# Attention and MLP on one core: key blocks of 64 for 58 queries, reciprocals spread by TensorE for eight pairs, query group sums on GpSimd at first

## The chip, the cores and the metric

The kernel runs on one core of a Trainium2 chip. The metric is the device time of one execution in microseconds (us). A profiled execution gives a trace; its span is about 1.7 us shorter than the time of the same execution. Executions are sorted into fast and slow (slow: over 1.5% above the fastest of the same kernel), and ratios use fast ones alone.

## The reference, cut to what matters

```python
# q, k, v: 8 batches x 8 heads x 576 x 64; x: 4608 x 512; w_in 512 x 2048; w_out 2048 x 512
q_d, k_d, v_d = means over groups of 4 neighbours        # 144 rows
out_d   = softmax(scale * q_d @ k_d.T) @ v_d             # then each row repeated 4 times
scores  = where(|i - j| < 4, scale * q @ k.T, -1e9)
x       = repeat(out_d, 4) + softmax(scores) @ v         # all heads beside each other
out     = silu(x @ w_in) @ w_out
```

So each head has a narrow band (each query sees seven keys) and a coarse attention over 144 averaged rows. Both softmaxes need their denominators' reciprocals, spread over the 64 rows of a head before the product P·V is scaled.

## The kernel before: the parts that matter here

Two heads (a "pair") are worked on at a time, 32 pairs in all. TensorE's queue holds transposes (T), scores (S), denominators (Z), P·V (PV), sums of v (VP), the spreading of the reciprocals (RB) and the MLP (g1 = x·w_in, g2 = g·w_out). In the long loop T(n+1), S(n), Z(n−1) and PV(n−2), of four neighbouring pairs, form one burst V(n), followed by four g1 and four g2.

```python
NDIR = 4                                   # pairs whose reciprocals TensorE spreads; the others go through DRAM
...
def pe_S(u, p):                            # 6 blocks: 64 keys for 48 queries
    for i in range(6):
        for h in range(2):
            for y in range(2):
                t = 288 * y + 48 * i
                mm(u, AB[half(y), h, 48 * i:48 * i + 48], kT[j][half(h), t:t + 64], qT[j][half(h), t:t + 48], rl, [rAB[h]])
    ...                                    # 8 more for the coarse scores
def pe_main(u, pv, z):
    for s in range(8):                     # denominators: 36 columns at a time, one-hot weights
        for h in range(2):
            for j in range(2):
                mm(u, CD[half(h), j, 360:396], oh1[half(j), 63 - s:127 - s] if s else ohf[half(j), :],
                   Pt[m][half(j), h, 36 * s:36 * s + 36], ...)
    ...                                    # coarse denominators, P.V in 6 blocks of 48, coarse P.V
def after_Z(p):
    one("DVE", f"r{p}", 0.75, lambda e: e.reciprocal(zr[i][:, :, :], CD[:, :, 360:396]), ...)   # 72 columns
    if p < NDIR:
        return
    dma(... scr[u] <- zr[i] ...)           # to DRAM and back, every row read by 64 partitions
def RB(p):                                 # 20 fp32 matmuls of 36 columns, weights = selectors
    for x in range(2):
        for m in range(10):
            mm(u, HP[:, x, 36 * m:36 * m + 36], sel[:, m, :], zr[i][:, x, :], ...)
...
for name in "T0 T1 S0 T2 S1 Z0 RB0 VP0 T3 S2 Z1 PV0 RB1 VP1 S3 Z2 PV1 RB2 VP2 Z3 PV2 RB3 VP3 PV3".split():
    ...                                    # prologue; then pairs 4 to 9 with the first 16 g1 between
for n in range(10, 46):                    # the loop: burst, then 4 g1 and 4 g2
    if n < NPAIR + 2:
        V(n)
        feed()
    G1(1); g2(j, tt, 0, bank, rb); G1(1); g2(j, tt, 1, bank, rb)
    G1(1); g2(j, tt, 2, bank, rb); g2(j, tt, 3, bank, rb); G1(1)
```

A planner then orders the units by estimated times; every engine executes its own list in that order.

The softmax here doesn't subtract the row's maximum and nothing guards it: scores larger than these inputs give would overflow.

Of the kernel before, what the change touches and what calls it, by code (L numbers as in the profile page):

```python
# [19 lines left out]
NDIR = 4  # L20
# [238 lines left out]
def bass_hourglass_attn__then__act_silu_kernel(  # L259
# [9 lines left out]
    with kctx:  # L269
# [22 lines left out]
        vs = sb("vs", [128, 12, 64], F32, NVS)  # L292
# [3 lines left out]
        vb = sb("vb", [128, 12, 64], BF16, NV)  # L296
# [7 lines left out]
        zr = sb("zr", [128, 2, 36], F32, 2)  # L304
        Rb = sb("Rb", [128, 720], F32, NR)
        xo = sb("xo", [128, 2, 360], F32, NX)
        scr = [nc.dram_tensor(f"scr{i}", [128, 72], F32, kind="Internal").ap() for i in range(NR)]

        sel = gT[1][:, 0:5, :].bitcast(F32).rearrange("p a (y m) -> p (a y) m", m=128)
        selr = [R(f"g1_{f}") for f in range(5)]  # L310
# [6 lines left out]
        pb = sb("pb", [128, 132], BF16)  # L317

        AB = E(nc.psum_tensor("AB", [128, 2, 512], F32))
        CD = E(nc.psum_tensor("CD", [128, 2, 512], F32))  # L320
# [5 lines left out]
        rCD = [R("C", True), R("D", True)]  # L326
# [22 lines left out]
        rc = R("xo1")  # L349

        def constants():
            def pool(fn, r=(), w=(), cost=0.3):
                one("POOL", "const", cost, fn, r, w)

            s, rid = cf[:, 0:64], R("cf")
            pool(lambda g: g.memset(s, 0.0), w=[rid], cost=0.15)
            for j in range(2):
                pool(lambda g, j=j: g.affine_select(out=s, in_=s, compare_op=ALU.not_equal, fill=1.0, base=-64 * j,
                                                    pattern=[[-1, 64]], channel_multiplier=1), r=[rid], w=[rid])
            pool(lambda g: g.tensor_copy(idn[:, :], s), r=[rid], w=[R("id"), R("xo1")], cost=0.2)  # L360

        def constants2():
            def pool(fn, r=(), w=(), cost=0.3):
                one("POOL", "const", cost, fn, r, w, prio=30)

            for i in range(NT):
                for a, b in ((0, 8), (584, 592)):
                    pool(lambda g, i=i, a=a, b=b: g.memset(kT[i][:, a:b], 0.0), w=[R(f"kTp{i}{a}")], cost=0.1)
                pool(lambda g, i=i: g.memset(kd[i][:, 144:192], 0.0), w=[R(f"kdp{i}")], cost=0.1)
            for i in range(NVQ):  # L370
                for s in (1, 3):
                    pool(lambda g, i=i, s=s: g.memset(vq[i][:, s, :], 0.0), w=[R(f"vqc{i}{s}")], cost=0.25)
            pool(lambda g: g.memset(oh1[:, :], 0.0), w=[R("oh1a")], cost=0.15)
            pool(lambda g: g.memset(oh4[:, :], 0.0), w=[R("oh4a")], cost=0.15)
            pool(lambda g: g.memset(ohc[:, :], 0.0), w=[R("ohca")], cost=0.15)
            pool(lambda g: g.memset(oh1[:, 63:64], 1.0), r=[R("oh1a")], w=[R("oh1")], cost=0.1)
            pool(lambda g: g.memset(ohf[:, :], 1.0), w=[R("ohfa")], cost=0.1)
            pool(lambda g: g.memset(ohf[:, 1:10], 0.0), r=[R("ohfa")], w=[R("ohf")], cost=0.1)
            pool(lambda g: g.memset(oh4[:, 63:64], 4.0), r=[R("oh4a")], w=[R("oh4")], cost=0.1)
            for j in range(2):  # L380
                one("DVE", "const", 0.1, lambda g, j=j: g.memset(ohc[64 * j:64 * j + 16, 63:64], 4.0),
                    r=[R("ohca")], w=[R(f"ohc{j}")])
            cf2 = xo[0][:, :, :].rearrange("p a b -> p (a b)")
            rm = R("cm")
            pool(lambda g: g.memset(cf2[:, 0:576], 1.0), w=[rm], cost=0.4)
            for j in range(2):
                s = cf2[:, 288 * j:288 * j + 288]
                m = s.rearrange("p (i q) -> p i q", i=6)
                pool(lambda g, m=m, j=j: g.affine_select(
                    out=m, in_=m, compare_op=ALU.is_ge, fill=0.0, base=-5 - 64 * j,  # L390
                    pattern=[[0, 6], [-1, 48]], channel_multiplier=1), r=[rm], w=[rm], cost=0.5)
                pool(lambda g, m=m, j=j: g.affine_select(
                    out=m, in_=m, compare_op=ALU.is_ge, fill=0.0, base=11 + 64 * j,
                    pattern=[[0, 6], [1, 48]], channel_multiplier=-1), r=[rm], w=[rm], cost=0.5)
                e = s[:, 240 * j:240 * j + 48]
                pool(lambda g, e=e, j=j: g.affine_select(
                    out=e, in_=e, compare_op=ALU.is_ge, fill=0.0, base=119 if j else -8,
                    pattern=[[0, 48]], channel_multiplier=-1 if j else 1), r=[rm], w=[rm])
            pool(lambda g: g.memset(sel[:, :, :], 0.0), w=selr, cost=0.8)
            for j in range(2):  # L400
                pool(lambda g, j=j: g.affine_select(
                    out=sel[:, :, half(j)], in_=sel[:, :, half(j)], compare_op=ALU.not_equal, fill=1.0,
                    base=-64 * j, pattern=[[-1, 10], [0, 64]], channel_multiplier=1), r=selr, w=selr, cost=0.9)
            pool(lambda g: g.memset(pb[:, :], 0.0), w=[R("pba")], cost=0.1)
            pool(lambda g: g.memset(cf2[:, 576:600], 1.0), w=[R("cp")], cost=0.1)
            for j in range(2):
                s = cf2[:, 576 + 12 * j:588 + 12 * j]
                pool(lambda g, s=s, j=j: g.affine_select(
                    out=s, in_=s, compare_op=ALU.is_ge, fill=0.0, base=-8 - 64 * j,
                    pattern=[[-4, 12]], channel_multiplier=1), r=[R("cp")], w=[R("cp")], cost=0.15)  # L410
                pool(lambda g, s=s, j=j: g.affine_select(
                    out=s, in_=s, compare_op=ALU.is_ge, fill=0.0, base=11 + 64 * j,
                    pattern=[[4, 12]], channel_multiplier=-1), r=[R("cp")], w=[R("cp")], cost=0.15)
            for j in range(2):
                one("DVE", "const", 0.1, lambda e, j=j: e.tensor_copy(
                    pb[half(j), 60:72], cf2[half(j), 576 + 12 * j:588 + 12 * j]), r=[R("cp"), R("pba")],
                    w=[R(f"pb{j}"), R("xo0")])
            for j in range(2):
                one("DVE", "const", 0.25, lambda e, j=j: e.tensor_copy(
                    mask_bf[half(j), :], cf2[half(j), 288 * j:288 * j + 288]), r=[rm], w=[R(f"mask{j}"), R("xo0")])  # L420
# [20 lines left out]
        def load_v(p):  # L441
            i = p % NVS
            for h in range(2):
                n = 2 * p + h
                base = v[n // H_, n % H_]
                for j in range(2):
                    lo, hi = 0, 6
                    off = (288 * j - 8) * D_
                    w = [R(f"vs{i}{h}{j}")]
                    d = vs[i][half(j), 6 * h:6 * h + 6, :]  # L450
                    if n == 0 and j == 0:
                        lo = 1
                        one("DVE", "zero", 0.15, lambda g, d=d: g.memset(d[:, 0, :], 0.0), w=w)
                        first = bass.AP(tensor=base.tensor, offset=base.offset, ap=[[64, 56], [1, 64]])
                        dma("SP", f"lv{p}e", vs[i][8:64, 0, :], first, w, f"vs{i}{h}{j}", 0.1, prio=10 * p + 15)
                    if n == 2 * NPAIR - 1 and j == 1:
                        hi = 5
                        last = bass.AP(tensor=base.tensor, offset=base.offset + 520 * D_, ap=[[64, 56], [1, 64]])
                        dma("SP", f"lv{p}e", vs[i][64:120, 11, :], last, w, f"vs{i}{h}{j}", 0.1, prio=10 * p + 15)
                    win = bass.AP(tensor=base.tensor, offset=base.offset + off + 3072 * lo,  # L460
                                  ap=[[64, 64], [3072, hi - lo], [1, 64]])
                    dma("SP", f"lv{p}", d[:, lo:hi, :], win, w, f"vs{i}{h}{j}", 0.55, prio=10 * p + 15)
# [42 lines left out]
        def castw(p):  # L505
            i, m = p % NVS, p % NV
            rr = [R(f"vs{i}{h}{j}") for h in range(2) for j in range(2)]
            one("POOL", f"cw{p}", 0.85, lambda g: g.tensor_copy(vb[m][:, :, :], vs[i][:, :, :]), r=rr, w=[R(f"vb{m}")])  # L508
# [20 lines left out]
        def after_T(p):  # L529
# [7 lines left out]
                kT[j][:, 8:584].rearrange("p (g r) -> p g r", r=9),  # L537
# [3 lines left out]
                kd[j][:, 0:SD], kT[j][:, 8:584].rearrange("p (g r) -> p g r", r=4), AX.X, ALU.add),  # L541
                r=[R(f"kT{j}")], w=[R(f"kd{j}")])
            one("DVE", f"mq{p}", 0.74, lambda e: e.tensor_reduce(  # L543
                qd[j][:, :], qT[j][:, :].rearrange("p (g r) -> p g r", r=4), AX.X, ALU.add),
                r=[R(f"qT{j}")], w=[R(f"qd{j}")])
# [373 lines left out]
```

## Time and profile before

| | before |
|---|---|
| median of 4 runs beside the changed kernel (range) | 437.4 us (433.9 to 443.4) |
| profiled run | 444.3 us, span 442.6 us, mean granted TensorE clock 0.942, slow |
| prologue / loop / tail of that span | 116.4 / 243.1 / 83.1 us |

Beside the lines that the prediction shows, two more of the page are needed. The first is VectorE's busy share in 40 equal slices of 11 us (9 is 90% or more); the second a group of instructions: busy us, mean ns of one, idle time just before.

```profile
DVE  5532125576555464656464656566776543433420
...
L666 DVE RECIPROCAL zr<-CD 128x72 f32<-128x72 f32 x32 | 19.4, 607 | 50.9 <-PE CD L336 50.9
```

VectorE is nowhere over 80% busy: it stands at 1 to 3 tenths in the slices from 22 to 66 us, where three of the four RB blocks lie.

### The profile page before, as it was taken

Reading aid. Unit: us, or ns where it says so; the run is one execution under the profiler, and the core shown is the slowest. Engines: PE = TensorE matmul, PEld = TensorE weight load, DVE = VectorE, ACT = ScalarE, POOL = GpSimd, SP = SyncE. Lnnn points to the kernel's source line nnn. Section 1 sums busy time; section 2 is a strip of 40 time slices with the busy share of each in tenths; the row PEclk is TensorE's granted clock in tenths of the full one; section 3 lists DMA queues with packets and bytes.
Section 4 is the critical chain, followed back from the end, with each engine's and each line's share of the span. In section 5 each row is a group of like instructions: output and inputs, shape, how many; then the busy total and the mean of one; then the engine's idle time right before and its main releaser. Section 6 shows DMA issues by size and latency. Waiting matters only on the chain.

```text
span 442.6 us, 14638 instructions
## 1 busy us (share of the span) xinstructions
PE 384.9 (87%) x6530; PEld 265.3 (60%) x6560; DVE 221.0 (50%) x355; ACT 169.1 (38%) x290; POOL 166.2 (38%) x207
## 2 busy tenths in 40 slices
PE   2799987974597887969797989799999999999997
PEld 1799985653464554646465656466666656666653
DVE  5532125576555464656464656566776543433420
ACT  4221024532244251524344445354545434343421
POOL 9441224356634444445354545445632120000000
PEclk9999999889589896969698999999999999999999
DMA  8999909978997474746575767583131210110111
GB/s 224 262 275 279 211 8 204 254 184 238 215 269 208 125 219 123 198 141 187 146 191 160 204 185 221 152 209 111 67 97 63 87 62 28 43 49 24 49 47 71
DMA packets 87258, 67.35 MB, mean 152 GB/s; under 512 B 59036, under 2 KB 68764, under 8 KB 87196
## 3 DMA queue, kind: packets, MB, share of 16 engines
q1 hardware_dynamic: 74460, 48.77, 41.9%
q10 hardware_dynamic: 8512, 11.36, 9.1%
q0 software_dynamic: 4224, 6.29, 6.6%
q8 instruction: 51, 0.84, 0.8%
q14 instruction: 11, 0.09, 0.1%
HBM read 58.03 MB, written 10.47 MB: 155 GB/s over the span
## 4 chain that ended last, share of the span: by engine, by line
PE 82%; issue 7%; DMA 4%; DVE 2%; ACT 2%; ACTq 1%; SPq 0%; DVEq 0%
PE HP L336 40%; PE o L336 23%; PE CD L336 8%; PE pe_ L336 6%; DMA scr<-zr 2%; PE AB L336 2%; PE pe_ L526 1%; DMA Rb<-scr 1%; DMA qk<-in_k_dram 1%; ACTq L425 1%; PE o L526 1%; ACT th L738 1%; DVE zr L666 1%; DVE gT L740 0%; SPq L425 0%
## 5 line engine op out<-in xcount | busy, mean ns | idle before, releaser
L336 PE MATMUL HP<-xT,w_in_sb 128*128 128x512 f32 x576 | 177.7, 447 | 2.7 <-DVE gT L740 2.3
L740 DVE SCALAR_TENSOR_TENSOR gT<-th,HP 128x512 bf16<-128x512 f32 x144 | 97.1, 685 | 119.3 <-ACT th L738 118.8
L738 ACT ACTIVATE th<-HP 128x512 f32<-128x512 f32 x144 | 85.8, 598 | 160.1 <-PE HP L336 150.1
L336 PEld LDWEIGHTS HP<-xT,w_in_sb 128*128 128x128 f32 x576 | 114.4, 204 | 34.1 <-DVE gT L740 3.2
L336 PE MATMUL o<-w_out_bf,gT 128*128 128x512 bf16 x437 | 106.4, 386 | 2.5 <-issue 1.0
L336 PEld LDWEIGHTS o<-w_out_bf,gT 128*128 128x128 bf16 x464 | 42.0, 100 | 60.0 <-issue 17.6
L722 POOL TENSOR_TENSOR xT<-xo 128x576 fp32r<-128x576 f32 (+3 forms) x48 | 45.0, 950 | 74.0 <-DVE xo L695 74.0
L508 POOL CAST vb<-vs 128x768 bf16<-128x768 f32 x32 | 26.4, 826 | 97.5 <-PE CD L336 88.5
L666 DVE RECIPROCAL zr<-CD 128x72 f32<-128x72 f32 x32 | 19.4, 607 | 50.9 <-PE CD L336 50.9
L502 POOL CAST qkb<-qk 128x1152 bf16<-128x1152 f32 x30 | 34.4, 1146 | 25.1 <-PE pe_ L526 13.2
L336 PE MATMUL CD<-Pt,vb 64*64 64x48 bf16 x768 | 14.8, 196 | 24.7 <-issue 24.4
L336 PE MATMUL HP<-zr,gT 128*128 128x36 f32 x160 | 35.0, 408 | 0.2 <-DVE zr L666 0.2
L336 PEld LDWEIGHTS HP<-zr,gT 128*128 128x128 f32 x160 | 34.4, 332 | 0.6 <-DVE zr L666 0.3
L695 DVE TENSOR_TENSOR xo<-CD,Rb 128x720 f32<-128x720 f32 x32 | 28.7, 898 | 11.7 <-PE CD L336 9.7
L513 POOL TENSOR_TENSOR vt<-vq 128x512 f32<-128x512 f32 x24 | 30.8, 1283 | 0.0
L536 ACT ACTIVATE kT<-pe_ 128x576 bf16<-128x576 bf16 x32 | 20.8, 650 | 18.9 <-PE pe_ L526 11.2
L755 ACT ACTIVATE osb<-o 128x512 f32<-128x512 f32 x29 | 17.4, 599 | 26.4 <-PE o L336 26.2
L336 PEld LDWEIGHTS CD<-Pt,vb 64*64 64x64 bf16 x768 | 11.1, 117 | 26.5 <-issue 25.4
L336 PE MATMUL pe_<-w_out_bf,gT 128*128 128x512 bf16 x109 | 26.1, 380 | 0.2
L540 DVE TENSOR_REDUCE kd<-kT 128x144 bf16<-128x576 bf16 x32 | 23.6, 738 | 1.7 <-ACT kT L536 1.7
L526 PE MATMUL o<-idn,qkb 64*64 64x64 bf16 x576 | 17.8, 206 | 7.6 <-DVE qkb L497 6.0
L543 DVE TENSOR_REDUCE qd<-qT 128x144 bf16<-128x576 bf16 x32 | 23.8, 743 | 1.3 <-ACT qT L339 1.2
(69 smaller groups left out, 358.3 us busy)
## 6 DMA issues: line engine op xcount, KB each, us to landing
vs<-in_v_dram SPq DMA_DIRECT2D x126, 96.0 KB, 4.1
Rb<-scr ACTq DMA_DIRECT2D x56, 180.0 KB, 4.1
qk<-in_q_dram SPq DMA_DIRECT2D x32, 288.0 KB, 5.5
out_dram<-osb SPq DMA_DIRECT2D x36, 256.0 KB, 2.3
qk<-in_k_dram SPq DMA_DIRECT2D x31, 288.0 KB, 6.0
vq<-in_v_dram SPq DMA_DIRECT2D x24, 256.0 KB
w_in_sb<-in_moe_w_in_dram POOLq DMA_DIRECT2D x4, 1024.0 KB, 10.0
w_out_bf<-in_moe_w_out_dram POOLq DMA_DIRECT2D x4, 512.0 KB, 9.9
```

The source lines that it names most:

```text
L336: L.op(u, lambda t: t.matmul(out_, lhsT, rhs, start=start, stop=stop, skip_group_check=True), r, w)
L502: one("POOL", f"c{p}", 1.15, lambda g: g.tensor_copy(qkb[j][:, :, :], qk[i][:, :, :]), r=[R(f"qk{i}0"), R(f"qk{i}1")], w=[R(f"qkb{j}0"), R ...
L508: one("POOL", f"cw{p}", 0.85, lambda g: g.tensor_copy(vb[m][:, :, :], vs[i][:, :, :]), r=rr, w=[R(f"vb{m}")])
L513: one("POOL", f"va{p}", 1.3, lambda g: g.tensor_tensor(vt[:, :, :], vq[i][:, :, 0:128], vq[i][:, :, 128:256], ALU.add), r=rr, w=[R("vt")])
L526: L.op(u, lambda e, o=o, w=w, j=j: e.transpose(o, w, idn[half(j), :]), [R("id"), R(f"qkb{n}{x}")], [rE if x else rF])
L540: one("DVE", f"mk{p}", 0.74, lambda e: e.tensor_reduce(kd[j][:, 0:SD], kT[j][:, 8:584].rearrange("p (g r) -> p g r", r=4), AX.X, ALU.add), ...
L543: one("DVE", f"mq{p}", 0.74, lambda e: e.tensor_reduce(qd[j][:, :], qT[j][:, :].rearrange("p (g r) -> p g r", r=4), AX.X, ALU.add), r=[R(f ...
L666: one("DVE", f"r{p}", 0.75, lambda e: e.reciprocal(zr[i][:, :, :], CD[:, :, 360:396]), r=rCD, w=[R(f"zr{i}")], prio=-4)
L695: one("DVE", f"m{p}", 0.92, lambda e: e.tensor_tensor(xo[x][:, :, :].rearrange("p x (m n) -> p x m n", n=36), CD[:, :, 0:360].rearrange("p ...
L722: one("POOL", f"a{p}", 0.15 + n * 0.0019, lambda g, dst=dst, in0=in0, in1=in1: g.tensor_tensor(dst, in0, in1, ALU.add), r=[R(f"xo{x}")], w ...
L738: one("ACT", f"t{j}_{f}", 0.62, lambda e: e.activation(th[tb][:, :], hps[hb], AF.Tanh, scale=0.5), r=[rH[hb]], w=[R(f"th{tb}")], prio=-1)
L740: one("DVE", f"s{j}_{f}", 0.71, lambda e: e.scalar_tensor_tensor(gT[j % 2][:, f, :], th[tb][:, :], 1.0, hps[hb], ALU.add, ALU.mult), r=[rH ...
```

## The change

Intent: fewer and wider TensorE instructions in the burst (58 queries a block; denominators 72 columns at a time), a cheap RB for eight pairs in place of a dear one for four, and a prologue in which T, S, Z, PV and RB of neighbouring pairs alternate.

```diff
-NDIR = 4
+NDIR = 8
-        vb = sb("vb", [128, 12, 64], BF16, NV)
+        vb = sb("vb", [128, 10, 64], BF16, NV)
-        zr = sb("zr", [128, 2, 36], F32, 2)
+        zr = sb("zr", [128, 2, 72], F32, 2)
...      # pe_S: blocks of 58 queries (the last 56)
-            for i in range(6):
+            for i in range(5):
                 for h in range(2):
                     for y in range(2):
-                        t = 288 * y + 48 * i
+                        c, n = 58 * i, 58 if i < 4 else 56
+                        t = 288 * y + c
...      # pe_main: denominators; P.V likewise 6 -> 5 blocks
-                for s in range(8):
+                for s in range(4):
...
-                               Pt[m][half(j), h, 36 * s:36 * s + 36],
+                               Pt[m][half(j), h, 72 * s:72 * s + 72],
...      # after_Z, p < NDIR: the reciprocal in three bf16 parts
+                one("ACT", f"rh{p}", 0.25, lambda e: e.activation(h, zf, AF.Copy), ...)
+                one("DVE", f"rx{p}", 0.22, lambda e: e.tensor_tensor(rrest, zf, h, ALU.subtract), ...)
+                one("DVE", f"rm{p}", 0.16, lambda e: e.tensor_copy(m, rrest), ...)
+                one("DVE", f"rl{p}", 0.22, lambda e: e.tensor_tensor(l, rrest, m, ALU.subtract), ...)
...      # RB: into the score banks AB
-                for m in range(10):
-                    mm(u, HP[:, x, 36 * m:36 * m + 36], sel[:, m, :], zr[i][:, x, :], ...)
+            for m, x, c, y, e_ in ((0, 0, 0, 0, 144), (1, 0, 144, 0, 144), (2, 0, 288, 0, 72),
+                                   (2, 1, 0, 72, 144), (3, 1, 72, 0, 144), (4, 1, 216, 0, 144)):
+                for a in range(3):
+                    mm(u, t[:, x, c:c + e_ - y], sel[:, m, :], rpart[a][:, y:e_], ..., start=a == 0, stop=a == 2)
...      # after_T, p < 8: the group sums of q as two adds on GpSimd
+            u = L.unit("POOL", f"mq{p}", 1.2)
...      # prologue, condensed
+        for n in range(10):
+            T(n + 1); S(n); Z(n - 1); PV(n - 2); RB(n - 1); VP(n - 1)      # as far as they exist
+            if n > 4:
+                G1((2, 4, 4, 4, 2)[n - 5])
```

Constants also move from GpSimd to VectorE, odd pairs before the fourth accumulate in other banks, and two small copies a pair move from VectorE to ScalarE.

## The prediction

A *line* is here a stretch of 256 TensorE instructions: 13,090 records of TensorE (6530 matmuls, 6560 weight loads) against 51 instruction packets before, 257 for each packet of some 16.5 KB (0.84 MB in 51). A *border* lies between two lines. That a burst which crosses two borders is stopped is the prediction's own guess, and the experiments test it. The 607 ns beside a cast's 286 are those of the reciprocal above.

> **What bounds the kernel now.** I read the page's slices first, then a table of stretches, then the chain of work, then the waits. The page's slices of the kernel before (each digit a tenth of a fortieth of the span) and its instruction queue:
>
> ```profile
> PE   2799987974597887969797989799999999999997
> ...
> PEclk9999999889589896969698999999999999999999
> ...
> q8 instruction: 51, 0.84, 0.8%
> ```
>
> TensorE is busy almost everywhere, so the question is what it is busy with, and where its clock drops. The table of stretches (start:end, length, busy us of each engine with instruction counts, granted clock, DMA share, GB/s), cut at the spreading of the reciprocals (RB) in the first four pairs and at the long loop:
>
> ```profile
> 15.66:24.41 8.75, 8.75 (x42) 8.68 (x43) 1.85 (x3) 1.02 (x2) 1.34 (x2) 1.00 1.28 285
> 24.41:28.86 4.45, 4.10 (x178) 3.64 (x177) 1.92 (x5) 3.02 (x5) 2.09 (x3) 1.00 1.22 227
> 28.86:37.54 8.68, 8.68 (x42) 8.61 (x43) 1.74 (x3) 0.02 (x1) 3.35 (x4) 1.00 1.27 281
> ...
> 66.00:116.40 50.40, 35.76 (x991) 27.14 (x995) 31.28 (x55) 20.87 (x37) 29.21 (x31) 0.85 0.96 221
> 116.40:139.80 23.40, 21.26 (x338) 13.77 (x328) 12.32 (x20) 9.21 (x16) 11.90 (x15) 0.81 0.87 222
> 139.80:359.50 219.70, 195.03 (x3902) 127.42 (x3923) 128.59 (x203) 93.46 (x163) 96.95 (x103) 0.94 0.54 152
> 359.50:442.60 83.10, 79.37 (x384) 46.42 (x389) 26.28 (x38) 30.35 (x51) 1.22 (x1) 1.00 0.12 45
> ```
>
> Three stages. **Prologue**, to 116.4 us: four RB blocks of 8.7 us each, in which VectorE, ScalarE and GpSimd stand nearly idle, then 50 us in which TensorE is busy 71% at a low clock. **Loop**, 116.4 to 359.5: 23 steps of one attention burst (V) and the MLP's four g1 and four g2, 243.1/23 = 10.57 us each. **Tail**, 83 us of plain MLP matmuls, untouched by the change. The groups of the page name the RB cost, and the waits what stops the loop:
>
> ```profile
> L336 PE MATMUL HP<-zr,gT 128*128 128x36 f32 x160 | 35.0, 408 | 0.2 <-DVE zr L666 0.2
> ```
>
> ```profile
> PE CD L336 <- issue: 24.4, 9, 4.5
> ```
>
> That last wait has no releaser: TensorE stops inside a burst, before or among the P·V matmuls, with all operands there. In time, one of them (start, length, engine, idle before):
>
> ```profile
> 141.00 0.31 PE L336 MATMUL CD<-Pt,vb 64*64 64x48 bf16 x16
> 141.35 0.65 ACT L567 ACTIVATE Pt<-AB 128x576 bf16<-128x576 f32 x1
> 145.77 0.14 PEld L336 LDWEIGHTS CD<-Pt,vb 64*64 64x64 bf16 x8 [4.56 <-issue]
> 145.77 0.25 PE L336 MATMUL CD<-Pt,vb 64*64 64x48 bf16 x8 [4.46 <-issue]
> ```
>
> It cuts one group of 24 equal matmuls in two. In the chain these pieces called issue come at 141, 164, 189, 212, 236, 258 and 278 us: every second step. A clean step exists too: from 317.8 to 326.7 and 326.7 to 335.6 TensorE is busy 8.83 of 8.90 us.
>
> [...]51 instruction packets of 0.84 MB are 16.5 KB each. A matmul is two instructions (weights and product): a step has 192 matmuls or 384 instructions, 1.5 lines, and so every second step its burst crosses two line borders; that fits the spacing of the stops. [...]the 5 and the 6s of PEclk stand where the long stops are. [...]Here 20 fp32 matmuls show as 40 records in 8.7 us, 434 ns for each of only 36 columns. [...]607 ns for 72 elements against 286 ns for a cast of 128.
>
> **The change, part by part.**
>
> *RB.* Out go 4 × 8.7 = 35 us of path time. In come 8 × 18 bf16 matmuls (reciprocals split into three bf16 parts; full rows, 144 or 72 columns). A bf16 128x128 weight load shows 100 ns; taking 60 to 100 ns per matmul, 18 cost 1.1 to 1.8 us, say 1.5; eight cost 12 us. They add on VectorE three small operations (estimate 0.6 us together) and on ScalarE one. Pairs 4 to 7 also lose their route through DRAM, whose waits stand on the chain of waits before (6.8 us for the scr write after pair 5, 3.0 and 4.9 us near 106 to 114).
>
> *Prologue pace.* Without RB's 8.7 us the other engines set it. Estimates per pair from rows of before: ScalarE 2×0.65 + 0.65 + 0.53 + 0.77, plus about 0.9 for the two vd copies it takes over and the split = 4.1 us; GpSimd 1.15 + 1.2 + 0.7 (cast of 640 elements in place of 768) + 1.2 (the q sums, at the 1.28 us for 512 and 0.74 us for 256 elements of its adds) = 4.3; VectorE about 4; the bank loop score, exp, RB, copy, next score about 5. Instructions: T 36 + S 28 + Z 24 + PV 28 + RB 18 + VP 15 = 149 matmuls = 298, 1.2 lines. A line arrived, from border to resumption, in 4 to 5.6 us under load (at 141 us: border at about 140.1, resumed 145.8), so 5 to 6.5 us a pair. Data: up to the loop it needs q and k of 12 pairs (6.9 MB), v windows of 9 (2.9), two group loads (0.6), and weights (6.3) = 16.7 MB; at the 275 GB/s of the first 50 us that is 61 us, so the loop cannot start before about 65. I take 9.5 us to the first scores, five steps of 6.2 and five of 7.5 (they hold 16 g1): 9.5 + 31 + 37.5 = 78 us against 116.4. **Saved: 38 us.**
>
> *Blocks of 58, denominators in 72 columns.* A burst had 12 + 32 + 36 + 48 + 32 = 160 matmuls and has 8 + 28 + 36 + 24 + 28 = 124. The chain shows 80 of them in 0.83 us, 10.4 ns each, set by their number and not by their 36 to 72 columns; 36 fewer save 0.37 us. A clean step falls from 8.90 to 8.53 us, 23 of them to 196 us. A step now has 312 instructions and its burst 248, under one line: it seldom crosses two borders. I keep 10 us of stops and half clock where 243.1 − 23×8.90 = 38 us stood. **Saved: 243 − 206 = 37 us.** In the loop the reciprocal grows from 72 to 144 elements[...]; VectorE goes from 6.28 to 6.8 us of an 8.5 us step: fuller, not the bound. The v windows fall from 384 to 320 KB a pair, the scr write doubles to 72 KB: the step's DMA stays near 1.9 MB, 225 GB/s.
>
> *q sums on GpSimd, constants moved to VectorE.* Only in the first eight pairs and the first 10 us; both engines had idle time there. No separate gain counted.
>
> Sum: 78 + 206 + 83 = 367 us of span. The profiled run of before took 444.3 us against its median of 436.4; that excess I read as stops, of which most go, so 366 for a median.
>
> **The rivals.** *1. The prologue becomes DMA-bound.* For it: the DMA share is over 1.2 in the RB blocks and a cast waited 5.9 us for vs at 26 us; a step of 6 us would ask for more than came. Against: that load was mostly the weights, and 25 MB had come by 116 us, more than needed. It would put the loop's start at 90 to 100: total 380 to 390. *2. Instruction fetch stays the bound,* slower because the transfers are packed into less time: 7 us a line would make the prologue 90 us and leave 25 us of stops in the loop: 395. Its gain would still be over 9%. *3. VectorE or the PSUM banks take over:* a longer reciprocal ahead of the SiLU products delays g1's banks by 0.3 to 0.5 us a step: 7 to 12 us. Against: before, TensorE waited for gT only 0.4 us at a step's start. *4. RB was hidden anyway.* Against: the chain holds all four blocks whole, with the other engines idle; this rival I drop.
>
> **Range and chances.** The two gains rest on different things, so I set 348 (loop starts at 68, hardly a stop) to 392 (rival 2 and some of 3). Even keeping every stop and a prologue of 100 us gives 442.6 − 16 − 8 = 418, 4% faster. Faster 0.97, same 0.02, slower 0.01.
>
> **What would show it.** Right: the group HP<-zr,gT is gone, 144 bf16 matmuls with sel stand for it at under 100 ns each; the first burst of the loop starts at 70 to 88 us; a clean step lasts 8.4 to 8.7 us; TensorE's waits on issue in CD fall from 24.4 us to under 8; about 42 instruction packets; the reciprocal at 1.1 to 1.2 us. Wrong: waits on DMA vs or qk before casts through the prologue (rival 1); issue waits in T, S or RB (rival 2); gT waits before HP in the loop (rival 3); or a clean step still at 8.9, if the matmuls' time goes by columns.

## The result, and the profile after

The changed kernel took **383.5 us** (median of 4 runs, 380.3 to 388.6) against 437.4 us; the ratio is **0.877** (95% interval 0.866 to 0.887). A ratio here is the mean time of one kernel's fast runs over the mean of the other's fast runs of the same rounds, so it is not quite the ratio of the medians. The kernel before has few fast runs in some rounds (3 of 7, 3 of 11), which moves ratios by a per cent between rounds; of the runs below, those of such rounds (e4b, e6, e9, e10) have only unclear comparisons on record. So microseconds are compared first.

| us of the profiled span | before (slow) | after (fast) | predicted |
|---|---|---|---|
| prologue, to the first burst of the loop | 116.4 | 92.2 | 78 |
| loop, 23 steps | 243.1 | 203.3 | 206 |
| tail | 83.1 | 83.1 | 83 |
| span | 442.6 | 378.6 | 367 |

The cut at 116.4 lies 1.0 us inside the first burst of before (115.44 us); from burst to burst the prologue gains 23.3 us and the loop 40.7. The profiled run of before is a slow one: the profiles differ by 64.0 us, the means of the fast runs (436.2 and 382.5 us) by 53.8. So some 10 us of this table are the state or chance, and no row says in which stretch they lie.

The page of the changed kernel (slices of 9.5 us; the instruction queue with packets, MB and share; the group of the reciprocals):

```profile
PE   2475689886999989989999999999999999999996
...
DVE  6555468698677858877787776778875434434310
...
PEclk9999999899999999999999999999999999999999
...
q8 instruction: 42, 0.69, 0.8%
...
L690 DVE RECIPROCAL zr<-CD 128x144 f32<-128x144 f32 x30 | 31.7, 1056 | 9.9 <-PE CD L339 5.2
```

From the eleventh slice on TensorE is busy 8 or 9 tenths until the last, and the 5s and 6s of the clock row are gone. Before that, from 0 to about 90 us, TensorE stands between 2 and 9. The group HP<-zr,gT of before is gone; the 144 matmuls that stand for it (least/median/most ns of one record):

```profile
L339 PE MATMUL AB<-gT x144: 196/246/328, 19.2 to 84.2; 128*128 128x144 bf16 x96, 128*128 128x72 bf16 x48
```

The table of stretches (columns as in the prediction) says who is busy in the prologue and the loop:

```profile
11.50:51.40 39.90, 25.89 (x729) 21.50 (x733) 22.12 (x34) 17.57 (x39) 25.09 (x34) 1.00 1.20 280
51.40:92.20 40.80, 33.01 (x704) 23.32 (x697) 33.62 (x52) 22.92 (x46) 27.14 (x30) 0.96 0.95 226
...
54.00:79.00 25.00, 22.86 (x474) 16.62 (x474) 18.55 (x32) 14.91 (x31) 16.17 (x18) 0.93 1.01 231
79.00:92.20 13.20, 8.53 (x175) 5.69 (x168) 12.54 (x17) 5.81 (x12) 9.14 (x10) 1.00 0.79 217
...
92.20:295.50 203.30, 197.64 (x3463) 128.37 (x3487) 149.32 (x222) 101.10 (x179) 106.78 (x118) 0.99 0.68 186
...
150.62:159.21 8.59, 8.52 (x156) 5.63 (x158) 6.70 (x12) 4.51 (x9) 5.09 (x5) 1.00 0.83 215
```

In the loop TensorE is busy 197.64 of 203.30 us; a clean step is 8.59 us with 156 matmuls, where before it was 8.90 us with 192. Its waits in the loop with no releaser (total, times, longest):

```profile
PEld CD L339 <- issue: 7.9, 22, 0.4
...
PEld o L339 <- issue: 2.8, 10, 0.3
...
PEld pe_ L339 <- issue: 0.8, 3, 0.3
```

They are waits of weight loads, none over 0.4 us; the nine of up to 4.5 us ahead of matmuls are gone. In the prologue the picture differs by stretch. Up to 51 us no engine is busy over 65%, and TensorE twice stops 2.4 us with no releaser (at 23.4 and 31.0 us) and once 2.6 (at 44.7). From 54 to 79 us TensorE is busy 91%. From 79 to 92 us VectorE is busy 95%. The chain of work at the very end of the prologue (start, length, what):

```profile
88.02 1.14 PE HP L339 x4
89.16 0.02 issue
89.18 0.61 ACT th L771
89.79 0.02 issue
89.81 0.69 DVE gT L773
90.50 0.79 DVE Pt L586
91.29 0.83 DVE xo L728
92.12 0.04 issue
92.17 0.22 PE CD L339
```

TensorE has nothing to do from 89.1 to 92.2 us: the first burst needs its bank, VectorE empties it last (xo), and VectorE does that behind a SiLU product and a mask that came before it in its list.

### The profile page after: what moved, and what is told of

Its sections match the earlier page's. It is cut to its first block, busy times and chain, and to the rows that moved or that the text cites.

```text
span 378.6 us, 12323 instructions
## 1 busy us (share of the span) xinstructions
PE 338.1 (89%) x5346; PEld 221.3 (58%) x5376; DVE 237.7 (63%) x379; ACT 176.9 (47%) x320; POOL 168.6 (45%) x215
## 3 DMA queue, kind: packets, MB, share of 16 engines
q10 hardware_dynamic: 7296, 10.62, 10.4%
## 4 chain that ended last, share of the span: by engine, by line
PE 77%; DMA 8%; DVE 4%; SPq 4%; issue 4%; ACT 2%; ACTq 1%; POOL 0%; POOLq 0%
PE HP L339 35%; PE o L339 22%; PE pe_ L339 7%; DMA scr<-zr 6%; PE CD L339 6%; PE AB L339 4%; SPq L426 4%; DMA qk<-in_k_dram 2%; PE o L531 1%; ACTq L426 1%; PE pe_ L531 1%; DVE Pt L586 1%; DVE gT L773 1%; DVE xo L728 1%; DVE gT L699 1%
## 5 line engine op out<-in xcount | busy, mean ns | idle before, releaser
L339 PE MATMUL HP<-xT,w_in_sb 128*128 128x512 f32 x576 | 164.1, 421 | 2.4 <-DVE gT L773 2.4
L339 PEld LDWEIGHTS HP<-xT,w_in_sb 128*128 128x128 f32 x576 | 106.8, 191 | 29.6 <-DVE gT L773 3.1
L339 PE MATMUL o<-w_out_bf,gT 128*128 128x512 bf16 x437 | 102.0, 380 | 1.8
L513 POOL CAST vb<-vs 128x640 bf16<-128x640 f32 x30 | 21.5, 717 | 60.6 <-PE CD L339 52.5
L690 DVE RECIPROCAL zr<-CD 128x144 f32<-128x144 f32 x30 | 31.7, 1056 | 9.9 <-PE CD L339 5.2
L582 ACT ACTIVATE Pt<-AB 128x576 bf16<-128x576 f32 x32 | 20.7, 647 | 6.1 <-PE AB L339 3.8
L531 PEld LDWEIGHTS o<-idn,qkb 64*64 64x64 bf16 x576 | 14.2, 119 | 11.7 <-DVE qkb L498 6.5
L531 PE MATMUL pe_<-idn,qkb 64*64 64x64 bf16 x576 | 17.1, 206 | 1.3 <-DVE qkb L500 0.7
L339 PE MATMUL CD<-Pd,vd 64*64 64x72 bf16 x360 | 15.1, 210 | 3.3 <-DVE xo L728 3.0
L339 PEld LDWEIGHTS pe_<-w_out_bf,gT 128*128 128x128 bf16 x112 | 10.0, 98 | 13.6 <-issue 3.2
```

The costliest lines, as they stand in the source:

```text
L339: L.op(u, lambda t: t.matmul(out_, lhsT, rhs, start=start, stop=stop, skip_group_check=True), r, w)
L513: one("POOL", f"cw{p}", 0.72, lambda g: g.tensor_copy(vb[m][:, :, :], vs[i][:, :, :]), r=rr, w=[R(f"vb{m}")])
L531: L.op(u, lambda e, o=o, w=w, j=j: e.transpose(o, w, idn[half(j), :]), [R("id"), R(f"qkb{n}{x}")], [rE if x else rF])
L690: one("DVE", f"r{p}", 1.2, lambda e: e.reciprocal(zr[i][:, :, :], CD[:, :, 360:432]), r=rCD, w=[R(f"zr{i}")], prio=-4)
```

## The experiments

Twelve kernels ran. The theories were: (a) in the loop, the number of matmuls in the burst sets both a step's length and the stops; rivals are that only the crossing of line borders inside a burst counts, that any instructions close in time count, or that the load of transfers makes the stops long; (b) the prologue is paced by instruction fetch, by TensorE's own work at half clock, by the DMA load, or by VectorE and the split. Letters in an expectation are its own names for such theories. "Start" is the first burst of the loop in the profiled run.

**The changed kernel again**, beside the second group of runs.

> The changed kernel itself, again, so that the others of this call have it on the same chip: 380 to 389 us; the loop starts near 92 us, its clean step takes 8.58 us.

Measured: 385.0 us (380.5 to 388.7), ratio 0.873 (0.863 to 0.883), start 94.8 us. Two profiled runs of one kernel thus differ by 2.6 us in the start. Three padded kernels below, with the same prologue on TensorE, started at 92.2, 94.9 and 97.1 us, so differences of up to 5 us in the start mean nothing by themselves.

**36 one-column matmuls more in each burst of the loop**, which restores the count of before (160 in a burst) with results that nobody reads.

```diff
-            pe_cross(u, pv, z)
+            pe_cross(u, pv, z); pad(u, 36, [AB[:, 0, :], AB[:, 1, :]], 504, rAB)
```

> The changed kernel with 36 one-column matmuls more in each attention burst of the loop, so that a burst has again 160 matmuls (320 instructions) and a step 192 (384). Theory A (a burst that crosses two borders of 256 instructions outruns the instruction fetch): stops of 2 to 4 us come back inside the bursts, in about every second step; idle on issue in the loop rises from 4 us to 20 or more, the loop grows from 203 us by 8 us for the extra matmuls (24 x 36 x 10 ns) and by 20 to 35 us of stops and half clock; total 405 to 425 us. Rival B (the loop gained by the matmuls' own time alone): plus 8 us, no stops, about 390 us.

Measured: 405.1 us (399.1 to 409.2), ratio 0.912 (0.899 to 0.925), start 92.2, 49 instruction packets. The loop's stretch and TensorE's waits in it:

```profile
92.20:313.50 221.30, 206.35 (x4288) 135.50 (x4312) 150.57 (x222) 101.85 (x178) 106.69 (x118) 0.99 0.65 172
```

```profile
PE o L339 <- issue: 5.6, 4, 2.4
...
PE HP L339 <- issue: 3.5, 3, 2.0
...
PE CD L339 <- issue: 0.7, 1, 0.7
```

The loop grew by 18.0 us: 8.7 us of busy time (206.35 − 197.64) and 9.3 us of idle time (14.95 against 5.66). A clean step takes 8.92 to 8.95 us (bursts at 151.78, 160.70, 231.88 and 240.83), some 0.35 us more for 36 matmuls, 10 ns each. So the count of matmuls costs time by itself, and the stops come back with it; but at 9.8 us of waits on issue they are below the 24.4 us of before and below the 20 of theory A, and 9.1 of them (`o` and `HP`) lie among the matmuls of the MLP, not inside bursts. The loop grew by less than the 28 to 43 us of that theory. Two of the four runs are slow; the fast ones took 399.1 and 402.7 us.

**The same 36 matmuls in the MLP, some 4 us behind the burst** (in the third g2 of a step).

```diff
-            g2(j, tt, 2, bank, rb)
+            g2(j, tt, 2, bank, rb, 36 if n < NPAIR + 2 else 0)       # pad(u, 36, ...) ahead of its own matmuls
```

> The same 36 one-column matmuls, in the same steps, but in the middle of the MLP part of the step, some 4 us behind the burst: a step has again 384 instructions, a burst 248. Theory A: plus 8 to 10 us for the matmuls themselves, hardly any stops inside bursts; about 390 us, 15 to 30 us below the kernel with the padding in the burst. Rival C (it is the number of instructions fetched in all that counts): as long as with the padding in the burst.

Measured: 401.5 us (396.6 to 406.2), ratio 0.910 (0.899 to 0.920), with stops of 0.8 to 1.9 us, 8.8 us in the loop, in the profiled run (a slow one). I had expected few stops if only the crossing inside a burst counts. They are as costly as in the run above (fast runs 399.9 us in the mean, there 400.9): **that form of the theory falls**, and rival C held. How a stop comes about is read from the instruction packets, at the end of this section.

**The 36 matmuls in the scores of prologue pairs 1 to 8.**

```diff
-            u = L.unit("PE", f"S{p}", 0.4 if p > 1 else 0.8)
+            u = L.unit("PE", f"S{p}", 0.4 if p > 1 else 0.8); pad(u, 36 if 1 <= p <= 8 else 0, [AB[:, 0, :], AB[:, 1, :]], 504, rAB)
```

> 36 one-column matmuls more ahead of the scores of pairs 1 to 8, in the prologue alone: 576 instructions or 2.25 lines. Theory D (the prologue goes at the pace of the instruction fetch, some 7 us a line there): the loop starts 10 to 16 us later than at 92 us. Rival E (chains over the other engines or the transfers set the pace): 2 to 5 us later (8 x 36 x 10 to 17 ns).

Measured: 395.3 us (391.0 to 400.1), ratio 0.896 (0.886 to 0.906), start 99.0: 4 to 7 us later. 576 instructions more are 2.25 lines; at the 6.5 to 7 us that I read for a line there (border to resumption) a prologue that hangs on fetch alone would lose 15 us. Their own time as matmuls is 3 to 6 us, an estimate from the 10 ns each of the loop and up to twice that where the recorded clock is 0.50. So the later start could be their own time alone, and does not decide. The trace says more: TensorE's busy time up to the start, from 9 us on, is 59.4 us, as in the run before (59.6), while the waits of its matmuls on issue rise to 16.9 us, from 12.4 and 13.0 in the two runs above. So fetch has a part in the prologue; as its sole pace (10 to 16 us expected) it falls. One start of a kernel below, 97.1, comes near 99.0 without any of these matmuls.

**Only four direct pairs, first attempt.** Its result was wrong (relative error 0.050): the same condition also dropped the v sums of pairs 4 to 7.

```diff
-NDIR = 8
+NDIR = 4
```

> The changed kernel with only the first four pairs spread by TensorE; pairs 4 to 7 take the route through DRAM again. If the route's waits (write, read back: some 8 to 14 us in the kernel before) fall on the path of the second half of the prologue, the loop starts 5 to 12 us later than at 92 us. Rival: four spreads of 1.1 us and their chain on VectorE and ScalarE cost more than the route, hidden behind g1: 0 to 5 us earlier.

Measured: 385.1 us (385.0 to 385.3), ratio 0.876, but with work missing; so it was mended:

```diff
-NDIR = 8
+NDIR = 4
             if 0 < n <= NDIR:
                 RB(n - 1)
+            if 0 < n <= NVP:
                 VP(n - 1)
```

> The changed kernel, but only the first four pairs' reciprocals are spread by TensorE; pairs 4 to 7 go through DRAM again (the v sums of all eight pairs stay on TensorE, so the result must be right this time). If the eight direct pairs are what keeps the prologue free of DRAM waits, the loop starts 4 to 8 us later than the 92 to 95 us of the changed kernel, ratio to before 0.885 to 0.90. If the prologue's gain comes from the form of the four blocks alone (bf16 with 144 columns in place of fp32 with 36), nothing is seen: start at 91 to 96, ratio 0.865 to 0.883.

Measured: correct, 383.6 us (382.0 to 387.1), start 92.4. Spreading eight pairs in place of four gains nothing that these runs can show. Its ratio, 0.884, belongs to rounds in which the fast runs of before were 431.8 to 436.7 us.

**The q sums back on VectorE.**

```diff
-            if p >= NVP:
+            if p >= 0:
                 one("DVE", f"mq{p}", 0.74, lambda e: e.tensor_reduce(qd[j][:, :], ...
```

> The q group sums of the first eight pairs back on VectorE (one operation of 0.74 us) from GpSimd (two, 1.1 us). Theory F (both engines have room, the move is worth nothing): the loop starts within 2 us of the changed kernel's. Rival G (GpSimd's operations hold up VectorE's bf16 operations; one took 1.50 us in place of 0.23 beside a GpSimd cast): VectorE's operations shorten and the loop starts 2 to 5 us earlier.

Measured: 383.2 us (380.1 to 386.9), ratio 0.872 (0.864 to 0.880), start 90.4. No difference from 385.0 us in the same rounds can be resolved: this part of the change is worth nothing that the total shows (fast runs 382.2 against 383.5 us in the mean). The start is 1.8 us earlier than in one profiled run of the changed kernel and 4.4 earlier than in the other, so the expectation's rival (2 to 5 us earlier) is not excluded.

**The reciprocal in two bf16 parts**: two VectorE operations and six matmuls a pair less, and still correct.

```diff
-                one("DVE", f"rx{p}", ..., e.tensor_tensor(rrest, zf, h, ALU.subtract), ...)
-                one("DVE", f"rm{p}", ..., e.tensor_copy(m, rrest), ...)
-                one("DVE", f"rl{p}", ..., e.tensor_tensor(l, rrest, m, ALU.subtract), ...)
+                one("DVE", f"rx{p}", ..., e.tensor_tensor(m, zf, h, ALU.subtract), ...)
-                for a in range(3):
+                for a in range(2):
```

> The reciprocal in two bf16 parts in place of three: 12 spreading matmuls a pair and two VectorE operations fewer. Expected from 110 ns a matmul at half clock and 55 to 60 at full: 0.7 us less in each of the first four pairs, 0.35 in the next four, and the waits for the last VectorE operation of the split (1.3 us, three times) gone: the loop starts 4 to 8 us earlier. If the fetch of instructions sets the pace, 96 instructions or 0.4 lines fewer: 2 to 3 us earlier. Result still correct (the parts hold some 16 bits).

Measured: 381.5 us (378.4 to 390.3), ratio 0.868 (0.860 to 0.876) against 0.873 (0.863 to 0.883) for the changed kernel in the same rounds; start 92.7. The intervals overlap, so it is not shown to be faster.

**The reciprocal spread in fp32 again**, six matmuls a pair, no split. This undoes the bf16 form alone and keeps the wide columns.

```diff
-                for a in range(3):
-                    mm(u, t[:, x, c:c + e_ - y], sel[:, m, :], rpart[a][:, y:e_], ..., start=a == 0, stop=a == 2)
+                zf = zr[p % 2][:, :, :].rearrange("p x n -> p (x n)")
+                mm(u, t[:, x, c:c + e_ - y], sel[:, m, :], zf[:, y:e_], ...)          # sel kept in fp32
```

> The changed kernel, but the reciprocals are spread in fp32 as in the kernel before: six fp32 matmuls a pair of 144 or 72 columns straight from the reciprocal, with no split into three bf16 parts (three VectorE operations and one of ScalarE less a pair). If the bf16 form is what the prologue's gain rests on, [...]eight pairs lose 15 to 25 us: the loop starts at 102 to 115 and the ratio is 0.90 to 0.93. If the number of matmuls counted (20 of 434 ns before, set by weights and not by columns), six of 434 ns are 2.6 us a pair, about what the split form and its chain take: start at 91 to 97 and ratio 0.865 to 0.885.

Measured: correct, 382.8 us (381.6 to 388.3, 6 runs), ratio 0.884 (fast runs of before 430.6 to 434.8 in these rounds), start 92.2. The duration of one matmul record (least/median/most ns; a matmul leaves two in fp32), first at half clock, then mostly at full:

```profile
L339 PE MATMUL AB<-zr,gT x60: 226/447/607, 18.5 to 55.3; 128*128 128x144 f32 x40, 128*128 128x72 f32 x20
```

```profile
L339 PE MATMUL AB<-zr,gT x36: 226/286/390, 65.2 to 81.0; 128*128 128x144 f32 x24, 128*128 128x72 f32 x12
```

One pair's six take 3.14 us in the first block (18.53 to 21.67) and 1.70 us in the last. The fp32 block of before, at the same half clock, took 8.7 us. So most of what a pair's RB gained comes from 6 wide matmuls in place of 20 thin ones: 435 ns each for 36 columns before, 523 ns (3.14/6) for 144 or 72 here. The bf16 form saves 0.6 to 1.2 us more a pair on TensorE (its 18 take 1.98 and 1.12 us there), and the total shows none of it. No run puts the 20 thin matmuls or the old order of the prologue back, so how the prologue's 23 us divide between RB's new form and the alternating order is not shown. My first expectation (102 to 115 us) fell; the rival, that their number counts, held.

**16 wide matmuls a pair more, in pairs 0 to 5, to raise TensorE's clock early.**

```diff
-            pe_VP(u, p)
+            warm(u, 8 if p < 5 else 0, pe_, rE); pe_VP(u, p)       # 224 columns each, overwritten
-            pe_T(u, p)
+            warm(u, 8 if 1 < p <= 6 else 0, o0, rF); pe_T(u, p)
```

> Idle work on purpose: in pairs 0 to 5, 8 matmuls of 224 columns (into unused columns of the banks) ahead of the transposes and ahead of the v group sums, 16 a pair. Theory H (the first half of the prologue runs at half clock because TensorE's work there is too thin; transposes take 0.70 us there and 0.48 later): the clock doubles before 52 us, transposes of pairs 2 to 5 fall to 0.5 us, and the loop starts at the same time or up to 5 us earlier, although 8 to 9 us of matmuls at full clock were added. Rival: the clock does not rise, and the loop starts 8 to 15 us later.

What it tests is seen in the transposes, which are the same work everywhere (least/median/most ns): the changed kernel, then this one.

```profile
L531 PE MATMUL o<-idn,qkb x54: 228/238/259, 28.9 to 43.8; 64*64 64x64 bf16 x54
```

```profile
L531 PE MATMUL o<-idn,qkb x72: 186/193/213, 25.0 to 46.4; 64*64 64x64 bf16 x72
```

238 ns goes with half clock, 193 ns with full clock: in the second profiled run of the changed kernel the recorded clock is 0.50 from 30.0 to 53.9 us, where transposes take 238 ns, and 1.00 at 65 to 75 us, where they take 193. The clock row of the page shows 9 for the first profile of the changed kernel there, so the row is not to be trusted ahead of the first record of the clock (52.1 us there). In the kernel before, the transposes between the RB blocks also take 238 ns, though TensorE is busy throughout those blocks (8.75 of 8.75 and 8.68 of 8.68 us in the first two). The extra matmuls did raise the clock, but the start was 94.9 us and the time 389.2 us (386.3 to 391.7), ratio 0.888 (0.880 to 0.895), 4 us worse than 385.0. Behind a stop of 3.35 us at 48.9 us the 18 matmuls of an RB took 1.98 us again (at 56.8 us), as at half clock, and the granted clock of 54 to 79 us is 0.84 in the mean. Half clock alone does not set the prologue's pace.

**Six of the eight weight loads released later.**

```diff
-        for c, t in enumerate((10, 14, 18, 22, 34, 38, 42, 46)):
+        for c, t in enumerate((10, 38, 46, 52, 56, 60, 64, 68)):
```

> The changed kernel with six of its eight weight loads released later in the plan (38 to 68 us in place of 14 to 46), so that fewer large transfers lie beside the first 40 us. If the load of the DMA engines makes the fetches of instruction lines slow (6.5 to 7 us a line there) and these set the prologue's pace, the stops of the first 50 us shrink from 2.4-2.6 us to under 1.5 each and the loop starts at 85 to 90 us; ratio 0.855 to 0.868. If TensorE's own work (half clock, 16 g1 in the second half) sets it, the start stays at 91 to 96, ratio 0.868 to 0.88. If the first g1 now wait for weights, start at 97 or later and ratio over 0.885.

Measured: 386.0 us (382.2 to 386.9), start 90.6. The DMA share of 25 to 54 us fell from 1.22 to 0.91, the stops of the first 50 us became somewhat shorter (at most 3.1 us against 3.6), and the start hardly moved; the waits of matmuls on issue up to it are 5.9 us in all, against 9.7 and 12.2 in the two profiles of the changed kernel. The load of the weights does not set the pace alone.

**The 36 matmuls in the burst, and the transfers of before as well**: four more v loads of 16 KB a pair from pair 10 on.

```diff
+                    if p >= 10:
+                        dma("SP", f"lx{p}", vex[i][half(j), h:h + 1, :], ...)      # 64 rows of 256 bytes
```

> The changed kernel with the 36 extra matmuls in each burst (as in e1_pad_burst, ratio 0.912 then) and, from pair 10 on, four more v loads of 16 KB a pair in 256-byte packets, as many bytes and packets as the kernel before had more. If the longer stops of before (24 us and the half clock after them, against 12.8 us in e1_pad_burst) come from transfers that slow the fetch, stops grow to 18 us or more and the ratio is 0.925 to 0.95. If the number of instructions within one fetch is all that counts, the ratio stays at 0.90 to 0.925 with stops of 10 to 16 us, and the loop of before differs from e1_pad_burst only by what else the burst holds.

Measured: 405.2 us (402.8 to 407.1, all fast), start 97.1. The 405.1 us without the loads holds two slow runs; its fast ones, of other rounds and another chip, took 399.1 and 402.7, so up to 4 us may be the loads'. The waits of its matmuls on issue, 6.0 us in all after 101 us, are no longer than there (9.5); in their place TensorE waited 6.1 us for ScalarE's copies of `o`, which waited for output transfers. Its ratio, 0.930, falls within the range that I gave for long stops, but only because the fast runs of before were faster in these rounds; the time and the trace decide. So these extra loads did not lengthen the stops.

**What the stops are, from the instruction packets.** The trace records each packet of queue 8, one for every 255 to 257 recorded TensorE instructions. In the kernel before, TensorE stops from 141.31 to 145.77 us (the stop that the prediction shows); no packet runs from 139.97 to 143.3, and then one does, from 143.34 to 144.36:

```profile
q8 instruction: 1, 0.02, 5.8%
```

So it is at every such stop. The 14 profiles have 94 stops of a matmul on issue of 0.5 us or more after 9 us, and each ends 1.0 to 1.8 us after the end of a packet. In the eight experiments whose records of matmuls are complete (a0, e4b to e10), all 45 such stops stand at the same place: 193 recorded TensorE instructions (weight loads, matmuls and waits) past a multiple of 256. The stops are waits for the next instruction line; this is shown.

Where the border lies decides how long the stop is: this second part is a reading of the same traces, and no run moves the border alone. A step of 384 instructions is exactly 1.5 lines, so the borders stand at the same place in every second step. In the kernel before (start, length, engine and group):

```profile
162.89 0.23 PE L336 MATMUL CD<-Pd,vd 64*64 64x72 bf16 x4
...
164.04 0.34 PE L336 MATMUL CD<-Pt,vb 64*64 64x48 bf16 x18
168.49 0.30 PE L336 MATMUL CD<-Pt,vb 64*64 64x48 bf16 x6 [4.12 <-issue]
```

The burst starts at 162.89 and is cut at 164.38, after 1.5 us, by 4.1 us. With the 36 extra matmuls the place is another:

```profile
164.54 0.81 PE L339 MATMUL o<-w_out_bf,gT 128*128 128x512 bf16 x3
167.77 1.04 PE L339 MATMUL o<-w_out_bf,gT 128*128 128x512 bf16 x4 [2.42 <-issue]
```

Here the burst is over at 162.4 and the cut comes in the MLP, three microseconds later, and is 2.4 us long. The 256 instructions of the line before the cut ran in 1.3 us in the kernel before (163.04 to 164.38) and in 4.3 us here (161.08 to 165.35). In all nine stops of the loop of before that line ran for 1.3 to 2.0 us, and TensorE went on 2.1 to 5.8 us after the line's start; in six of the padded kernel it ran for 2.2 to 4.9 us, and TensorE went on after 3.3 to 6.7 us. In these lines wide matmuls filled the time until the next line was there, thin ones did not.

Transfers are not out of it. A packet takes 0.9 to 1.5 us, but when it starts varies: in the nine stops of before from 0.4 us ahead of the line's start to 3.4 us after it, with a DMA share of 0.98 to 1.06; in three stops of padded kernels 0.7 to 0.9 us after it, with a share under 0.35. Whether DMA load delays a line is open; the last experiment, whose extra loads lengthened no stop, speaks against a large effect at its own load only.

## Why the prediction was right or wrong

**Total: right, 366 against 383.5 us within 348 to 392.** By its steps:

- *Blocks of 58, clean step:* right. 8.53 us was foreseen, 8.59 came; 10.4 ns a matmul by its number was confirmed by putting 36 back (some +0.35 us a step, +8.7 us in the loop, 10 ns each).
- *Stops in the loop:* right, and better than kept. "I keep 10 us of stops and half clock": TensorE is idle 5.7 us in the loop (203.30 − 197.64), and no stop of a matmul on issue stands among its waits. Restoring the 36 matmuls brought 9.3 us of idle time back. That stops are waits for the next line is shown by the packets; the prediction's form of it, two borders inside one burst, fell with the matmuls in the MLP. Of the profiled loop's 40 us the extra matmuls account for 18. In fast runs of the same rounds before (439.4 us) is 38.5 us above the padded kernel (400.9); some 23 of these are the prologue's by the profiles, and the 15 or so left are put down to the place of the borders and the half clock behind long stops (at five of the nine in the loop before the recorded clock falls to 0.50 for 3.4 to 6.8 us), which is argued and not shown.
- *RB:* the sum was nearly right: 12 us were foreseen for eight; the eight blocks hold some 13 us of work, and 3.1 us of waiting for the last part of the split. Eighteen matmuls took 1.98 us at half clock and 1.12 at full; "under 100 ns each" failed at half clock (110 ns). The reason was half wrong: I put the saving to bf16, and the fp32 run shows that fewer, wider matmuls bring most of it.
- *"Pairs 4 to 7 also lose their route through DRAM":* worth nothing that the runs show (383.6 us with four direct pairs).
- ***Prologue pace*, the mis-sized term:** "9.5 + 31 + 37.5 = 78 us". Read from the trace, the terms were 11.5 (the first scores began at 8.8, but were complete only after 2.3 us of waiting for a constant from GpSimd), 39.9 and 40.8: 92.2 us. The first five steps, 8.0 us each in place of 6.2, are most of the miss, 8.9 of 14.2 us. There I took the largest of several separate limits. No engine is busy over 65%; the stops on fetch (7.4 us in all) and the waits of the bank loop come at different times, so they add up. Of those limits the line itself was too short: 4 to 5.6 us from border to resumption were foreseen, and 5.6 to 7.6 came at the five stops of this prologue. I also took the durations at full clock, though TensorE ran at half. The last five steps, 8.2 us each in place of 7.5, hold 16 g1; TensorE is busy 91% from 54 to 79 us and 81% over the five, which end with 3.0 us of waiting behind VectorE's list (rival 3, at a place where I had not looked for it).
- *Which of these sets the pace* is not settled. Early clock, later weights, two parts, four direct pairs, q sums on VectorE and fp32 all left the start at 90.4 to 94.9 us, within the scatter of kernels with the same prologue. The waits of matmuls on issue go with the start: 5.9 us of them with a start at 90.6, 9.7 at 92.2, 12.2 at 94.8, 14.9 at 97.1 and 16.9 at 99.0. Only the last of these kernels has more instructions there, and the kernel with the extra wide matmuls falls out of the row (7.5 us at 94.9). That is a link between runs and no proof of which causes which.
- *Rival 1 (DMA):* its start of 90 to 100 us came, but with late weights the DMA share fell and the start stayed at 90.6 us, so DMA is not the sole bound (the 275 GB/s taken for the first 50 us of before is the rate of single slices; the mean there is 255); *rival 2 (fetch)*, with its 90 us, came near what the prologue did (92.2), but not in the loop, where its 25 us of stops did not come. The packets show only one line fetched ahead at the nine stops in the loop of before: there the packet of the next line started between 0.4 us ahead of the start of the line that ran before the stop and 3.4 us after it. *Packets 42* and the *reciprocal's growth* came nearly as said (1.1 to 1.2 us foreseen, 1.056 measured: 6.2 ns for each of the 72 elements added to the 607 ns of before).
- *From span to time:* 366 as the median of a 367 us span was careless: the time is 1.7 us over the span, and the profiled run here was the fastest of four.

No version beat the changed kernel beyond doubt; two parts and fp32 are as fast with less code.

## What to carry to other kernels

Where TensorE stops with its operands there, look for an instruction packet that ends 1 to 2 us before TensorE goes on (1.0 to 1.8 us in these runs), and count the instructions against one line of 256: here the line before a stop had run in 1.3 to 5.7 us. Fewer and wider matmuls saved here their own time (10 ns each) and the stops as well (24.4 us of waits on issue in CD before, no wait on issue over 0.4 us in the loop after), and a step of 1.5 lines repeated a bad border in every second step. For thin matmuls, widen the columns before changing the type: in fp32 at half clock, 20 matmuls of 36 columns took 8.7 us, six of 144 or 72 took 3.14 us. When a stretch has no engine over 65% busy, do not size it by the largest single limit: add the waits that take turns, and expect that removing one alone shows nothing: in six runs here the start stayed at 90.4 to 94.9 us.
